# Inverse transform over k2: one F32 product or three 12-bit F32R products, from the seventh group on

## The chip, the cores and the metric

One core of a Trainium2 chip runs the kernel. The metric is the time of one launch on the device in microseconds (us), the median of several runs. The profile is of one execution, taken by the hardware profiler; its times count from the start of its span. Engines: TensorE (PE, with PEld for its weight loads), ScalarE (ACT), VectorE (DVE), GpSimd (POOL), and SyncE (SP), which issues the DMAs.

## The reference

The input x is 2 sequences of 3008 tokens with 256 features. Three layers follow each other:

```python
X = np.fft.rfft(x, axis=1)
Yr = Xr @ w_r - Xi @ w_i + b_r
Yi = Xr @ w_i + Xi @ w_r + b_i
Y = shrink(Yr) + 1j * shrink(Yi)        # towards zero by 0.01
y = np.fft.irfft(Y, n=3008, axis=1)
h = y @ win1;  x1 = (h * cos(h)) @ wout1        # 256 -> 2048 -> 256
h = x1 @ win2; out = (h * clip(h + 3, 0, 6) / 6) @ wout2
```

All inputs and the output are float32 (the weights of the last two layers come as float64).

## The kernel before

**Precision.** Most products on PE are made from split operands. A value is written once to the type F32R (a float with 12 mantissa bits that are kept, the high part), and once as the rest, value minus high part, in F32R too. A product is then three: high x high, high x low, low x high, added in PSUM. Products of the two long transforms over k2 aren't split: both operands are F32, and an F32 product is executed as two passes on PE.

**First phase, to about 165 us.** The transform of 3008 tokens is done in two steps (47 x 64). `a_part` makes the forward step, `w_mm`, `b_mm`, `v_mm` the rest up to `u`, which goes to DRAM (`u_dram`) in 96 rows for each of 32 pairs of columns and both sequences. Meanwhile a converter, spread in small steps between the other work, turns the float64 weights into split F32R tiles: `load` fetches 512 KB into one of two buffers with the tag `raw`, ACT, DVE and POOL work on it, and the last reader of a raw tile is line 169 on DVE. The converter does the second layer's weights during the second phase.

**Inverse step.** A group is four pairs, 376 tokens; there are 16 groups (0 to 15). `load_u(g)` fetches u (96 x 4 x 256) and the table tg (96 x 376) for one group into one buffer each. `y_part(g, ec)` makes one half of the 256 features of the group: four products of 96 rows, 128 x 94 (line 290), into one PSUM tile of the tag `h`, of which there are four buffers. ACT and DVE then write the result as high and low part into the token tiles (lines 304 and 305). After the second half it calls `load_u(g + 1)`. Groups 0 to 2 are done in the first phase, the others in the second.

**Second phase.** The tokens are 12 blocks of up to 512. A unit is 128 of the 2048 hidden features of one block and layer. `mm_h` makes it on PE (line 602, six products of 512 columns into an `h` tile); ACT and DVE apply the function (lines 613, 614, 626, 634, 635 for layer 0, lines 618 and 637 for layer 1) and split it (`gh`, line 645 on ACT, `gl`, line 646 on DVE, which is the last reader of the `h` tile); `mm_out` multiplies it by wout four units later (line 659, six products). Units of layer 0 (even) and layer 1 (odd) alternate, a group of 32 units for each block, so that layer 1 is three blocks behind. In a unit's turn ACT gets, in this order, the first function of this unit, `gh` of the unit two before, the second function of the unit before, and, in layer 0, line 626 of this unit. The order on PE, ACT and SP is the program's; DVE and POOL are put in order by a planner.

**Where the inverse step stands.** The parts of the groups that the next block needs are hung behind units near the end of the present group of units, in a table `events`: the last part three units before the end, the others two units apart in front of it. Four of the 16 groups (7 and 8, 11 and 12) are needed in pairs; the others of the groups 6 to 15 singly.

Of the kernel before, what the change touches and what calls it, by code (L numbers as in the profile page):

```python
# [9 lines left out]
F32 = mybir.dt.float32  # L10
F32R = mybir.dt.float32r
# [3 lines left out]
AF = mybir.ActivationFunctionType  # L15
ALU = mybir.AluOpType
# [5 lines left out]
NB, D, DFF = 2, 256, 2048  # L22
# [4 lines left out]
TP = 2 * N1  # L27
ROWS = 2 * DOF
LAM = 0.01
TWO_PI = 2.0 * math.pi  # L30
YPAIRS = 4
# [3 lines left out]
TILE = 128  # L35
# [9 lines left out]
STAGED = [0] * 9 + [1, 2, 4, 5, 7, 8, 10] + [12] * 10  # L45
YP = (15, 17, 18, 19, 20, 21, 22)
YE = 3


def _split(a):  # L50
# [66 lines left out]
def fourier_moe_moe_kernel(ctx, tc, x, w_r, w_i, b_r, b_i, ta, tg, fg, win1, wout1, win2, wout2, out):  # L117
    nc = tc.nc
    pe, act, dve, sp = nc.tensor, nc.scalar, nc.vector, nc.sync

    def f32(ap):
        return ap.bitcast(F32)

    persist = ctx.enter_context(tc.tile_pool(name="persist", bufs=1))
# [130 lines left out]
    MAXT = max(BLOCK_TOKENS)  # L255
    starts = [sum(BLOCK_TOKENS[:j]) for j in range(NBLK + 1)]
    YT = YPAIRS * TP
    NG = NB * NPAIR // YPAIRS

    def tok0(j):  # L260
# [2 lines left out]
    def groups_of(j):  # L263

        return range(-(-starts[j] // YT), -(-starts[j + 1] // YT))

    u_sb, tg_sb, y_sb, x1_sb = {}, {}, {}, {}


    def token_sets(pool, i, tag):  # L270
# [5 lines left out]
    def load_u(g):  # L276
        if g >= NG:
            return
        b, p0 = divmod(g * YPAIRS, NPAIR)
        ut = persist.tile([ROWS, YPAIRS, D], F32, tag="u_sb", name=f"u_sb{g}")  # L280
        sp.dma_start(ut, u_dram[b][:, :, p0 : p0 + YPAIRS, :].rearrange("s f i e -> (s f) i e"))
        tt = persist.tile([ROWS, -(-YT // TILE) * TILE], F32, tag="tg_sb", name=f"tg_sb{g}")
        sp.dma_start(tt[:, 0:YT], tg[:, p0 * TP : (p0 + YPAIRS) * TP])
        u_sb[g], tg_sb[g] = ut, tt

    def y_part(g, ec):

        yp = psum.tile([128, 512], F32, tag="h", bufs=4, name=f"yp{g}_{ec}")
        for i in range(YPAIRS):
            pe.matmul(  # L290
                yp[:, i * TP : (i + 1) * TP],
                lhsT=u_sb[g][:, i, ec * 128 : (ec + 1) * 128],
                rhs=tg_sb[g][:, i * TP : (i + 1) * TP],
                start=True,
                stop=True,
            )
        for j in range(NBLK):
            t0, t1 = max(g * YT, starts[j]), min((g + 1) * YT, starts[j + 1])
            if t0 < t1:
                if j not in y_sb:  # L300
                    y_sb[j] = free_sets.pop(0)
                yh, yl = (z[:, t0 - starts[j] : t1 - starts[j]] for z in y_sb[j][ec])
                src = yp[:, t0 - g * YT : t1 - g * YT]
                act.activation(yh, src, AF.Copy)  # L304
                dve.tensor_tensor(yl, src, f32(yh), op=ALU.subtract)
        if ec == 1:
            load_u(g + 1)


    with ExitStack() as actx:  # L310
        apool = actx.enter_context(tc.tile_pool(name="apool", bufs=1))
        with tc.manual_schedule(engines={mybir.EngineType.PE, mybir.EngineType.SP, mybir.EngineType.Activation}):
# [238 lines left out]
            for i in range(NB * NP):  # L551
                k2_step(i)
                if i == 0:
                    constants(2)
                if i == YP[0]:
                    free_sets += token_sets(persist, 0, "zt")
                    load_u(0)
                elif i in YP:
                    y_part(*divmod(YP.index(i) - 1, 2))
# [5 lines left out]
    mpool = ctx.enter_context(tc.tile_pool(name="mpool", bufs=1))  # L565
    with tc.manual_schedule(engines={mybir.EngineType.PE, mybir.EngineType.SP, mybir.EngineType.Activation}):
# [5 lines left out]
        order, units, events = [], [], {}  # L572
        for i, group in enumerate(groups):
            g0, n0 = len(units), len(order)
            order += group
            step = 4 if i == 0 else 1
            for q in range(NFC // step):
                units += [(n0 + n, *job, q * step + f) for n, job in enumerate(group) for f in range(step)]
            size = len(units) - g0
            if i + 1 < len(groups) and groups[i + 1][0][0] == 0:  # L580
                parts = [(g, e) for g in groups_of(groups[i + 1][0][1]) for e in range(2)]
                for k, (g, e) in enumerate(reversed(parts)):
                    events.setdefault(g0 + size - YE - 2 * k, []).append(lambda g=g, e=e: y_part(g, e))

        acc, hp_t, gs_t, mid = {}, {}, {}, {}
        w2i, w2o = None, None
# [98 lines left out]
        for g in range(G + DELAY):  # L685
# [22 lines left out]
            if 0 <= g - DELAY < G:  # L708
                n2, m2, _, fc2 = units[g - DELAY]
# [50 lines left out]
```

## Time and profile before

| | |
|---|---|
| three runs | 1225.84, 1227.66, 1229.45 us; median 1227.66 us |
| the profiled execution | 1225.41 us, of which the span from the first to the last instruction is 1223.6 us |
| PE busy | 1216.1 us (99%) |
| DVE, ACT, POOL busy | 803.1, 786.0, 86.1 us |
| granted clock of PE | full in all 40 slices |

The busy times are sums over the span. Matmuls on PE are pipelined: one begins before the one before it has ended, so a matmul's own duration is longer than the distance to the next one's start, and it is the distance that PE's stream is made of.

### The profile page before, as it was taken

To read this page: it belongs to the slowest core of one execution; us is meant where nothing else is said; L and a number is where in the kernel's file an instruction comes from. 1 tells how busy PE (TensorE), PEld (TensorE's weight loads), DVE (VectorE), ACT (ScalarE), POOL (GpSimd) and SP (SyncE) were. 2 spreads that over 40 slices of the span, in tenths; PEclk is the share of its full clock that TensorE was granted. 3 is DMA by queue.
4 is the path that set the end of the run, shared out by engine and by line. 5 is a ranking of instruction groups with operands and counts; after the bars stand their busy time and mean duration, and the time that the engine had idled before them with its cause. 6 is when DMAs were issued, how large, how long until landed. Compare 5 with 4: busy or idle time off the path is not lost.

```text
span 1223.6 us, 15626 instructions
## 1 busy us (share of the span) xinstructions
PE 1216.1 (99%) x5671; PEld 1021.2 (83%) x5673; DVE 803.1 (66%) x1328; ACT 786.0 (64%) x1487; POOL 86.1 (7%) x68
## 2 busy tenths in 40 slices
PE   8999999999999999999999999999999999999998
PEld 7888878888888888888888888888888888888888
DVE  3978789899986655656566556656556656554444
ACT  3667689898776666666666666666666666654443
POOL 0330122222321000000000000000000000000000
PEclk9999999999999999999999999999999999999999
DMA  9633431212200001000001001001001000000000
GB/s 247 190 97 94 129 96 52 70 54 70 69 36 18 18 1 36 18 1 18 18 1 35 1 19 35 1 1 35 1 1 35 1 1 18 1 1 18 18 8 23
DMA packets 25077, 48.47 MB, mean 40 GB/s; under 512 B 2756, under 2 KB 12744, under 8 KB 25000
## 3 DMA queue, kind: packets, MB, share of 16 engines
q1 hardware_dynamic: 25000, 47.48, 13.5%
q8 instruction: 44, 0.72, 0.2%
q14 instruction: 33, 0.27, 0.1%
HBM read 35.02 MB, written 12.45 MB: 39 GB/s over the span
## 4 chain that ended last, share of the span: by engine, by line
PE 95%; DVE 1%; DMA 1%; ACT 1%; issue 0%; SPq 0%; DVEq 0%
PE acc L659 41%; PE h L602 41%; PE pp L422 5%; PE bp L447 3%; PE yp L290 2%; PE zp L349 1%; PE vp L473 1%; DMA x_big<-in_x_dram 1%; DMA x<-in_x_dram 1%; PE bp L442 0%; DVE r L614 0%; DVE h L635 0%; DVE gl L646 0%; SPq L342 0%; SPq L338 0%
## 5 line engine op out<-in xcount | busy, mean ns | idle before, releaser
L637 DVE SCALAR_TENSOR_TENSOR h<-r,h 128x512 f32<-128x512 f32 (+1 forms) x192 | 131.3, 684 | 251.3 <-ACT r L618 251.2
L602 PE MATMUL h<-tok,w1i 128*128 128x512 f32 (+1 forms) x1152 | 291.6, 388 | 1.0 <-DVE gl L646 0.5
L602 PE MATMUL h<-tok,w2i 128*128 128x512 f32 (+1 forms) x1152 | 287.8, 385 | 0.0
L659 PE MATMUL acc<-gh,w1o 128*128 128x512 f32 (+1 forms) x768 | 264.5, 385 | 0.0
L659 PE MATMUL acc<-gh,w2o 128*128 128x512 f32 (+1 forms) x768 | 263.6, 385 | 0.0
L646 DVE TENSOR_TENSOR gl<-h,gh 128x512 fp32r<-128x512 f32 (+1 forms) x384 | 258.0, 672 | 0.6 <-ACT gh L645 0.5
L602 PEld LDWEIGHTS h<-tok,w1i 128*128 128x128 f32 x1152 | 213.1, 188 | 44.1 <-DVE gl L646 2.1
L602 PEld LDWEIGHTS h<-tok,w2i 128*128 128x128 f32 x1152 | 214.8, 188 | 41.0 <-DVE gl L646 0.4
L645 ACT ACTIVATE gh<-h 128x512 fp32r<-128x512 f32 (+1 forms) x384 | 224.5, 585 | 4.8 <-DVE h L635 3.8
L618 ACT ACTIVATE r<-h 128x512 f32<-128x512 f32 (+1 forms) x192 | 113.0, 588 | 172.9 <-PE h L602 172.9
L614 DVE SCALAR_TENSOR_TENSOR r<-r,h 128x512 f32<-128x512 int32 (+1 forms) x192 | 129.5, 675 | 103.3 <-ACT r L613 103.1
L613 ACT ACTIVATE r<-h 128x512 int32<-128x512 f32 (+1 forms) x192 | 113.0, 589 | 130.8 <-PE h L602 129.7
L659 PEld LDWEIGHTS acc<-gh,w1o 128*128 128x128 f32 x768 | 144.0, 188 | 27.9
L659 PEld LDWEIGHTS acc<-gh,w2o 128*128 128x128 f32 x768 | 143.9, 188 | 27.4
L659 PE MATMUL acc<-gl,w1o 128*128 128x512 f32 (+1 forms) x384 | 147.8, 385 | 0.0
L659 PE MATMUL acc<-gl,w2o 128*128 128x512 f32 (+1 forms) x384 | 147.8, 385 | 0.0
L626 ACT ACTIVATE r<-r 128x512 f32<-128x512 f32 (+1 forms) x192 | 119.7, 623 | 42.5 <-DVE r L614 41.7
L635 DVE TENSOR_TENSOR h<-r,h 128x512 f32<-128x512 f32 (+1 forms) x192 | 129.3, 674 | 0.0
L634 ACT ACTIVATE r<-r 128x512 f32<-128x512 f32 (+1 forms) x192 | 120.0, 625 | 0.0
L659 PEld LDWEIGHTS acc<-gl,w1o 128*128 128x128 f32 x384 | 72.1, 188 | 13.9
L659 PEld LDWEIGHTS acc<-gl,w2o 128*128 128x128 f32 x384 | 72.1, 188 | 13.9
L304 ACT ACTIVATE tok<-yp 128x376 fp32r<-128x376 f32 (+22 forms) x54 | 19.2, 356 | 31.1 <-PE yp L290 20.6
(89 smaller groups left out, 907.8 us busy)
## 6 DMA issues: line engine op xcount, KB each, us to landing
u_dram<-v SPq DMA_DIRECT2D x48, 128.0 KB, 2.4
u_sb<-u_dram SPq DMA_DIRECT2D x16, 384.0 KB, 3.8
out_dram<-o SPq DMA_DIRECT2D x22, 256.0 KB, 2.1
x<-in_x_dram SPq DMA_DIRECT2D x11, 384.0 KB, 5.0
raw0i<-in_win_dram SPq DMA_DIRECT2D x8, 512.0 KB, 3.9
raw0o<-in_wout_dram SPq DMA_DIRECT2D x8, 512.0 KB, 4.1
raw1i<-in_win_dram SPq DMA_DIRECT2D x8, 512.0 KB, 3.6
raw1o<-in_wout_dram SPq DMA_DIRECT2D x8, 512.0 KB, 3.7
```

Source lines behind the costliest of these rows:

```text
L422: pe.matmul(pp.rearrange("p a e -> p (a e)"), lhsT=za[:, p, kc, 2 * (k2 % 2) : 2 * (k2 % 2) + 2, :].rearrange("p r n -> p (r n)"), rhs=wb[ ...
L602: pe.matmul(hp[:, :t], lhsT=w[:, c0 : c0 + 128], rhs=r[:, :t], start=(i == 0), stop=(i == 5))
L613: act.activation(k[:, :t], hp[:, :t], AF.Copy, bias=0.0, scale=1.0 / TWO_PI)
L614: dve.scalar_tensor_tensor(r[:, :t], k[:, :t], -TWO_PI, hp[:, :t], op0=ALU.mult, op1=ALU.add)
L618: act.activation(r[:, :t], hp[:, :t], AF.Relu, bias=3.0, scale=1.0)
L626: act.activation(mid[g][:, :t], mid[g][:, :t], AF.Abs)
L634: act.activation(r[:, :t], r[:, :t], AF.Sin, bias=math.pi / 2, scale=-1.0)
L635: dve.tensor_tensor(hp[:, :t], r[:, :t], hp[:, :t], op=ALU.mult)
L637: dve.scalar_tensor_tensor(hp[:, :t], r[:, :t], 6.0, hp[:, :t], op0=ALU.min, op1=ALU.mult)
L645: act.activation(gh[:, :t], hp[:, :t], AF.Copy)
L646: dve.tensor_tensor(gl[:, :t], hp[:, :t], f32(gh[:, :t]), op=ALU.subtract)
L659: pe.matmul(acc[n][d][:, :t], lhsT=w[:, fc % 2, d * 128 : (d + 1) * 128], rhs=r[:, :t], start=(fc == 0 and i == 0), stop=(fc == NFC - 1 an ...
```

## The change

For groups 6 to 15 (`YR = 6`) u and tg are split as other operands are. A new function `split_u(g)` lets ACT write the high parts and POOL the low parts of both: u's into two tiles of the tag `raw`, whose buffers the converter used until then, tg's into two new tiles. Then it calls `load_u(g + 1)`, which for these groups is no longer called by `y_part`. `y_part` makes three F32R products where it made one F32 product: high x high, high x low, low x high, added in PSUM. The events: the two halves of a group stay two units apart; where two groups are needed for a block, the first of them stands 12 units ahead of the second (it was 4); `split_u(g)` stands five units before the group's first half. Groups 0 to 5 are as before.

```diff
+YR = 6
...
+    TGW = -(-YT // TILE) * TILE
...
+    def split_u(g):
+
+        us_sb[g] = [persist.tile([ROWS, YPAIRS, D], F32R, tag="raw", bufs=2, name=f"us{z}_{g}") for z in range(2)]
+        tgs_sb[g] = [mpool.tile([ROWS, TGW], F32R, tag=f"tgs{z}", name=f"tgs{z}_{g}") for z in range(2)]
+        for src, (hi, lo) in ((u_sb[g], us_sb[g]), (tg_sb[g][:, 0:YT], [t[:, 0:YT] for t in tgs_sb[g]])):
+            act.activation(hi, src, AF.Copy)
+            nc.gpsimd.tensor_tensor(lo, src, f32(hi), op=ALU.subtract)
+        load_u(g + 1)
+
     def y_part(g, ec):
 
         yp = psum.tile([128, 512], F32, tag="h", bufs=4, name=f"yp{g}_{ec}")
+        if g < YR:
+            terms = [(u_sb[g], tg_sb[g])]
+        else:
+            (uh, ul), (th, tl) = us_sb[g], tgs_sb[g]
+            terms = [(uh, th), (uh, tl), (ul, th)]
         for i in range(YPAIRS):
-            pe.matmul(
-                yp[:, i * TP : (i + 1) * TP],
-                lhsT=u_sb[g][:, i, ec * 128 : (ec + 1) * 128],
-                rhs=tg_sb[g][:, i * TP : (i + 1) * TP],
-                start=True,
-                stop=True,
-            )
+            for k, (u, t) in enumerate(terms):
+                pe.matmul(
+                    yp[:, i * TP : (i + 1) * TP],
+                    lhsT=u[:, i, ec * 128 : (ec + 1) * 128],
+                    rhs=t[:, i * TP : (i + 1) * TP],
+                    start=(k == 0),
+                    stop=(k == len(terms) - 1),
+                )
...
-        if ec == 1:
+        if ec == 1 and g < YR:
             load_u(g + 1)
...
                 for k, (g, e) in enumerate(reversed(parts)):
-                    events.setdefault(g0 + size - YE - 2 * k, []).append(lambda g=g, e=e: y_part(g, e))
+                    at = g0 + size - YE - (2 * k if g < YR else 2 * (1 - e) + 12 * (k // 2))
+                    events.setdefault(at, []).append(lambda g=g, e=e: y_part(g, e))
+                    if g >= YR and e == 0:
+                        events.setdefault(at - 5, []).append(lambda g=g: split_u(g))
```

## Rows read from the trace of the kernel before

**Rows 1.** The page: the span, and busy time and instructions of each engine.

```profile
span 1223.6 us, 15626 instructions
...
PE 1216.1 (99%) x5671; PEld 1021.2 (83%) x5673; DVE 803.1 (66%) x1328; ACT 786.0 (64%) x1487; POOL 86.1 (7%) x68
```

**Rows 2.** The page: the chain that ended last, by line.

```profile
PE acc L659 41%; PE h L602 41%; PE pp L422 5%; PE bp L447 3%; PE yp L290 2%; PE zp L349 1%; PE vp L473 1%; DMA x_big<-in_x_dram 1%; DMA x<-in_x_dram 1%; PE bp L442 0%; DVE r L614 0%; DVE h L635 0%; DVE gl L646 0%; SPq L342 0%; SPq L338 0%
```

**Rows 3.** The view of line 290: durations min/median/max in ns.

```profile
L290 PEld LDWEIGHTS yp<-tg_sb,u_sb x256: 187/192/192, 126.0 to 1010.4; 96*128 96x128 f32 x128
L290 PE MATMUL yp<-tg_sb,u_sb x256: 244/275/275, 126.2 to 1010.5; 96*128 96x94 f32 x128
```

**Rows 4.** PE in order of time about group 10's first half: start, us.

```profile
643.71 0.39 PE L659 MATMUL acc<-gl,w2o 128*128 128x512 f32 x1
...
644.62 0.39 PE L659 MATMUL acc<-gh,w2o 128*128 128x512 f32 x1
644.85 1.03 PE L290 MATMUL yp<-tg_sb,u_sb 96*128 96x94 f32 x8
645.72 1.66 PE L602 MATMUL h<-tok,w1i 128*128 128x512 f32 x6
647.22 0.39 PE L659 MATMUL acc<-gh,w1o 128*128 128x512 f32 x1
...
648.58 1.52 PE L602 MATMUL h<-tok,w2i 128*128 128x512 f32 x6
649.94 0.39 PE L659 MATMUL acc<-gh,w2o 128*128 128x512 f32 x1
```

**Rows 5.** PE and its weight loads in order of time, 645.26 to 645.95.

```profile
645.26 0.61 PE L290 MATMUL yp<-tg_sb,u_sb 96*128 96x94 f32 x4
...
645.40 0.30 PEld L290 LDWEIGHTS yp<-tg_sb,u_sb 96*128 96x128 f32 x2
645.72 0.30 PEld L602 LDWEIGHTS h<-tok,w1i 128*128 128x128 f32 x2
```

**Rows 6.** DVE in order of time, beside the same part.

```profile
644.98 0.68 DVE L646 TENSOR_TENSOR gl<-h,gh 128x512 fp32r<-128x512 f32 x1
```

**Rows 7.** PE in order of time about a part of the first phase (group 2).

```profile
149.89 1.03 PE L290 MATMUL yp<-tg_sb,u_sb 96*128 96x94 f32 x8
150.70 0.47 PE L422 MATMUL pp<-wh,zh 128*128 128x512 f32 x1
...
152.16 0.40 PE L473 MATMUL vp<-sh,fgr 128*128 128x512 f32 x1
```

**Rows 8.** PE in order of time in the last block: 384 columns.

```profile
1101.31 0.33 PE L659 MATMUL acc<-gh,w1o 128*128 128x384 f32 x1
...
1102.19 0.34 PE L659 MATMUL acc<-gh,w1o 128*128 128x384 f32 x1
```

**Rows 9.** Groups by form: a copy from SBUF on ACT, a subtraction on POOL.

```profile
L173 ACT ACTIVATE w2o<-cva1o 128x512 fp32r<-128x512 f32 x8 | 5.1, 631 | 0.0
...
L176 POOL TENSOR_TENSOR w2o<-cva1o,w2o 128x512 fp32r<-128x512 f32 x8 | 10.4, 1294 | 22.2 <-ACT w2o L173 22.2
```

**Rows 10.** ACT in order of time: idle before and its releaser in brackets.

```profile
643.75 0.60 ACT L618 ACTIVATE r<-h 128x512 f32<-128x512 f32 x1 [0.80 <-PE h L602]
```

**Rows 11.** The view of line 646, from 300 to 376 us.

```profile
L646 DVE TENSOR_TENSOR gl<-h,gh x28: 676/683/692, 302.1 to 375.6; 128x512 fp32r<-128x512 f32 x28
```

**Rows 12.** DVE, POOL and PE in order of time before group 6's first half.

```profile
358.31 0.69 DVE L169 SCALAR_TENSOR_TENSOR cvb1o<-raw1o,cvb1o 128x512 f32<-128x512 uint32 x1
...
369.19 0.69 DVE L169 SCALAR_TENSOR_TENSOR cvb1o<-raw1o,cvb1o 128x512 f32<-128x512 uint32 x1
...
370.02 1.31 POOL L170 TENSOR_TENSOR cva1o<-cva1o,cvb1o 128x512 f32<-128x512 f32 x1 [8.33 <-DVE cvb1o L169]
...
375.49 1.03 PE L290 MATMUL yp<-tg_sb,u_sb 96*128 96x94 f32 x8
```

**Rows 13.** The page: DMA issues, the load of u.

```profile
u_sb<-u_dram SPq DMA_DIRECT2D x16, 384.0 KB, 3.8
```

More of the change, by code (lines that the diff above doesn't have):

```diff
@@ L267, in fourier_moe_moe_kernel @@
     u_sb, tg_sb, y_sb, x1_sb = {}, {}, {}, {}
+    us_sb, tgs_sb = {}, {}
     def token_sets(pool, i, tag):
@@ L281, in load_u @@
         sp.dma_start(ut, u_dram[b][:, :, p0 : p0 + YPAIRS, :].rearrange("s f i e -> (s f) i e"))
-        tt = persist.tile([ROWS, -(-YT // TILE) * TILE], F32, tag="tg_sb", name=f"tg_sb{g}")
+        tt = persist.tile([ROWS, TGW], F32, tag="tg_sb", name=f"tg_sb{g}")
         sp.dma_start(tt[:, 0:YT], tg[:, p0 * TP : (p0 + YPAIRS) * TP])
         u_sb[g], tg_sb[g] = ut, tt
+    def split_u(g):
[5 more added lines that the diff above has]
+        load_u(g + 1)
     def y_part(g, ec):
         yp = psum.tile([128, 512], F32, tag="h", bufs=4, name=f"yp{g}_{ec}")
-        for i in range(YPAIRS):
-            pe.matmul(
-                yp[:, i * TP : (i + 1) * TP],
-                lhsT=u_sb[g][:, i, ec * 128 : (ec + 1) * 128],
-                rhs=tg_sb[g][:, i * TP : (i + 1) * TP],
-                start=True,
-                stop=True,
-            )
+        if g < YR:
[3 more added lines that the diff above has]
+            terms = [(uh, th), (uh, tl), (ul, th)]
+        for i in range(YPAIRS):
+            for k, (u, t) in enumerate(terms):
[6 more added lines that the diff above has]
+                )
         for j in range(NBLK):
```

## The prediction

> **What bounds the kernel.** I read the page's first lines: TensorE (PE) is busy for 1216.1 of 1223.6 us [rows 1]. Then the chain that ended last: PE's lines L659 and L602 are 82% of it, and the line the change rewrites, L290, 2% [rows 2]. So nearly every microsecond added to PE's stream is added to the end, and one taken from it is won only if nothing else holds PE at that place. L290 shows 256 PE instructions for 16 groups x 2 halves x 4 = 128 products: an F32 product is two passes of 94 columns, each with a weight load [rows 3].
>
> Next I read one part's place in order of time: group 10's first half, between two groups of six at L602 [rows 4]. Its eight passes start at 644.85, the next L602 matmul at 645.72: 0.87 us. The six matmuls there take 1.50 (645.72 to 647.22), where the six at 648.58 take 1.36 (to 649.94). A part thus costs 0.87 + 0.14 = 1.01 us. The pace of the passes is that of the weight loads: two loads in a row span 0.30 at about 0.19 each, so start to start is 0.11, and four passes of 0.275 span 0.61, so 0.112 from start to start [rows 3, 5]. Two loads of L602, which are F32R, span 0.30 too: an F32R load isn't faster.
>
> Then VectorE. The gl of L646 runs 644.98 to 645.66 [rows 6], and L602's next matmul and weight load start together at 645.72 [rows 4, 5]. gl ends the use of an h buffer in PSUM, and a part takes a fifth tile from these four buffers. So after its last pass PE waits some 0.06 us for gl, though no view lists it (PE is still counted busy). The first six parts show the case without gl: the eighth pass starts about 0.75 after the first (1.03 less 0.275) [rows 3, 7], the next matmul 0.81 after the first (149.89 to 150.70), and the six after it take 1.46 (to 152.16) [rows 7]. From a part's first pass to the end of the next six that is 2.27, against 2.37 (644.85 to 647.22) here. The gate costs 0.10 us a part. It also sets a floor: shorter products would leave L602 at 645.72.
>
> **The change part by part.** *Products.* For groups 6 to 15, in 2 halves each, so 20 parts, 8 passes become 4 x 3 = 12 passes of F32R with 94 columns. No row of before shows an F32R product under 384 columns. Bounds: from above, 0.176 at 384 columns (1101.31 to 1102.19 in five) [rows 8], unless a narrow F32R product goes as an F32 one does, 2 x 0.112 = 0.224. From below, the line through 384 (0.176) and 512 columns (0.228: 643.71 to 644.62 in four [rows 4]) carried down to 94 columns gives 0.176 - 290 x 0.052/128 = 0.06. In between lies 0.11, at which F32R loads follow each other [rows 5]; since every product here loads its own 128 columns of weights, and the three terms reload uh rather than keep it (PE has 5673 loads for 5671 matmuls [rows 1], though L602 uses weights twice in a row), I take 0.112. That products accumulate into the same 94 columns costs nothing at this pace: the two F32 passes do so now.
>
> Sum for a part: four more passes x 0.112 = +0.45, first pass to next matmul 0.81 + 0.45 = 1.26, and the six after it 1.46; together 2.72 for today's 2.37. That is +0.35: 0.45 less the gate's 0.10, since L602 then asks for its buffer at 646.11, after gl's 645.66. Twenty parts: +7.0 us. With the bounds: with p a product's pace, the first pass to the next matmul is 0.81 + 12p - 8 x 0.112 = 12p - 0.09, and the change a part is that + 1.46 - 2.37: at 0.176, +1.11, in all +22; at 0.224, +1.69, +34; at 0.06 the gate holds, +0.
>
> The Trainium skill, "TensorE: Matmul & The Clock Gate", section LDWEIGHTS, says that a weight load's time goes by its columns, columns / 1.2 in ns, whatever the contraction: 107 ns here. By that page an estimate of the sum is 20 x 4 x 0.107 = 8.5 us less the gate: the trace's 0.112 agrees, and the rule speaks against trading two loads for three.
>
> *Splits.* Ten times ScalarE copies 1024 and 376 elements. A copy from SBUF takes 0.63 at 512 [rows 9], so these at most 1.26 and 0.63, 1.89 together. They stand behind L626 of an even unit, and before the next instruction, L618 of the odd unit, ScalarE is idle for 0.80, until PE has ended L602 [rows 10]. So 0.80 is covered, and L618, the gh behind it and the gl that frees an h buffer come up to 1.1 later. What covers that: gl ends 1.9 us after L618's start (643.75 to 645.66 [rows 6, 10]), and without a part in between PE asks for that buffer only after the six products of L659 (1.36) and the whole next unit (647.22 to 649.94, 2.72 [rows 4]), some 4 us after L618's release, which leaves 2 us. Bound: 0 to 1.1 a split, 0 to 11 us; I take 0, as the 2 us are more. GpSimd subtracts 1024 and 376 elements; at 1.29 for 512 [rows 9] at most 2.6 and 1.3. Copies and subtractions take at most 5.8 us, and the part follows five units or 5 x 2.72 = 13.6 us later: covered. GpSimd costs VectorE nothing that I can see: a gl takes 0.683 in the median while GpSimd converts [rows 11], and 0.68 where it is idle [rows 6].
>
> *Buffers.* The halves of u go into the converter's raw buffers. Before group 6 the last raw tile is read until 369.88 (369.19 + 0.69), and the split is due five units before the part, near 362. The copy uses the older buffer, last read at 359.0 (358.31 + 0.69); GpSimd's first subtraction waits to 369.9, and at 3.9 both end at 373.8, or at 376.5 if two operations of the conversion (from 370.02, 1.31 and 1.29) go first. The part starts at 375.49 [rows 9, 12]: 0 to 1.0 us, once. I take 0, as the subtractions are due first. Behind GpSimd's wait stand only the last conversions.
>
> *Loads.* The next group's load moves from behind a part to behind its split, 12 units or more ahead of use, and takes 3.8 us [rows 13]. On SP it waits for GpSimd, and the next output stores behind it are far off. Nothing.
>
> *Moved parts.* Where a block needs two groups, the first's parts move 8 units earlier, behind an odd unit as now; the same gate, the same cost. Nothing.
>
> So 1225.41 + 7.0 = 1232.4 for the profiled execution; it lies 2.25 under the median 1227.66, and the forecast for a median is 1234.7.
>
> **Rivals.** *A. The forecast*, 0.112 a product: +7.0; own range with the scatter of the three runs, 1231 to 1238. Chance 0.74.
>
> *B. No change*, the other side: if a narrow F32R product goes at its columns' rate (0.06), the part ends before gl, and L602 starts at 645.72 as now. It decides from 12p - 0.09 under 0.87, so p under 0.08: 1227.7. For it: the line through 384 and 512 columns. Against it: loads at 0.11 after each other. Chance 0.10. [...]
>
> *C. Narrow F32R is dearer than its load*, 0.176 to 0.224: +22 to +34, 1250 to 1262. For it: no row shows F32R so narrow. Against it: the F32 passes reach 0.112. Chance 0.08.
>
> *D. The splits stall PE*: ScalarE's 1.1 passes on to PE by gl at half or more of the 10 splits: +7.0 and 5 to 11, 1240 to 1246. It decides where gl comes over 2 us late. For it: ScalarE runs in order, and gh stands behind the copies. Against it: those 2 us. Chance 0.08.
>
> **How the numbers follow.** A measurement of this kernel tells 0.3%, 3.7 us, from no change. A, C and D are slower except for an edge of A; of B a fifth could be measured as faster. Slower 0.87, same 0.10, faster 0.03. The range leaves out C, most of B and the far end of D: 1230 to 1243.
>
> **What would show it.** L290 in groups 6 to 15 with 240 instead of 160 passes, each shorter than the 0.275 of now, starts 0.11 apart, 1.26 from a part's first pass to L602, six at L602 in 1.46 and 0.35 more from part to part. B: L602 still starts 0.06 after gl. C: starts 0.176 or more apart. D: PE idle before L602 with gl late, or before L290 in group 6 with GpSimd as what ended it. The forecast is wrong if F32R loads of 94-column products don't follow each other at 0.11.

## The result

The changed kernel takes 1235.91 us (median of 14 runs), the kernel before 1228.72 us (median of 14), a ratio of 1.0065 with a 95% interval of 1.0051 to 1.0079. It is slower by 7.2 us; the forecast was 7.0 us, 1234.7 us for the median and 1230 to 1243 as its range. Of the 1.2 us between 1234.7 and 1235.91, 1.06 are there because the kernel before has a median of 1228.72 here and had 1227.66 in the three runs that the forecast started from.

The page of the changed kernel, as [rows 1, 2] of before; line 680 is what was 659, 623 was 602, 308 was 290, 667 was 646:

```profile
span 1235.6 us, 15858 instructions
...
PE 1227.2 (99%) x5751; PEld 1031.8 (84%) x5753; DVE 804.3 (65%) x1328; ACT 798.7 (65%) x1507; POOL 119.8 (10%) x88
...
PE acc L680 41%; PE h L623 40%; PE pp L440 5%; PE yp L308 3%; PE bp L465 3%; PE zp L367 1%; PE vp L491 1%; DMA x_big<-in_x_dram 1%; DMA x<-in_x_dram 1%; PE bp L460 0%; DMA tg_sb<-in_tg_dram 0%; DVE r L635 0%; DVE h L656 0%; DVE gl L667 0%; SPq L360 0%
```

PE has 80 matmuls more, 20 parts of 12 instead of 8, as many more loads, and it still sets the end. This execution's span is 12.0 us longer than that of before, and not all of that is the change: PE in order of time at the first part that the change touches (group 6's first half):

```profile
380.17 0.39 PE L680 MATMUL acc<-gh,w2o 128*128 128x512 f32 x1
380.40 1.44 PE L308 MATMUL yp<-tgs,us 96*128 96x94 f32 x12
```

Its first pass starts at 380.40, in before at 375.49 [rows 12]. So 4.9 us were lost earlier, and all of it by 142.9 us, long before the first instruction that the change touches (the copy on ScalarE at 367.53). PE, early in the changed kernel's span (367 was 349, 440 was 422):

```profile
23.32 1.91 PE L367 MATMUL zp<-ta,x 96*128 96x96 f32 x8 [1.86 <-DMA x<-in_x_dram]
...
27.96 0.63 PE L440 MATMUL pp<-wl,zh 128*128 128x512 f32 x1
28.39 0.63 PE L440 MATMUL pp<-wh,zl 128*128 128x512 f32 x1
```

PE had waited 1.86 us for x (1.39 at the same place in before), and from 23.3 to 30 us its granted clock was 0.51, about the lower of its two levels (1.2 of 2.4 GHz), where it was 1.00 in before: products of L440 start 0.43 apart, the same ones in before 0.23. By then 3.6 us are lost; the rest is lost by 142.9 us, where PE waited 0.9 us for a load of tg. A later run with the same splits and buffers, e8 below, has a granted clock of 1.00 in those stretches and starts that part at 376.33. From that part's first pass to the span's end the changed kernel takes 855.2 us, before 848.1: 7.1 us for 20 parts, 0.355 each. The runs of before scatter in the same way: beside e1 to e4, 13 of them with a mean granted clock of 0.997 took 1229.9 us in the mean, 7 with 1.0 took 1226.9.

One part, the counterpart of [rows 4 to 6]: PE, its weight loads and VectorE in order of time at group 10's first half, then the view of line 308 as in [rows 3].

```profile
652.61 1.44 PE L308 MATMUL yp<-tgs,us 96*128 96x94 f32 x12
653.88 1.61 PE L623 MATMUL h<-tok,w1i 128*128 128x512 f32 x6
655.34 0.40 PE L680 MATMUL acc<-gh,w1o 128*128 128x512 f32 x1
...
653.51 0.41 PEld L308 LDWEIGHTS yp<-tgs,us 96*128 96x128 f32 x3
...
652.75 0.68 DVE L667 TENSOR_TENSOR gl<-h,gh 128x512 fp32r<-128x512 f32 x1
```

```profile
L308 PEld LDWEIGHTS yp<-tgs,us x240: 188/192/192, 380.2 to 1022.6; 96*128 96x128 f32 x120
L308 PE MATMUL yp<-tgs,us x240: 208/274/276, 380.4 to 1022.6; 96*128 96x94 f32 x120
```

Three loads span 0.41 at 0.19 each: 0.11 from start to start, the pace of before. The first pass to L623 takes 1.27 (0.87 in before), the six matmuls there 1.46 (1.50): 2.73 against 2.37, 0.36 a part. All 20 parts of the changed kernel take 2.73, those of before 2.36 to 2.38. gl is over at 653.43, and L623 starts 0.45 later: it waits no more.

### The profile page after: what moved, and what is told of

The parts are those of the page before. It is cut to its first block, busy times and chain, and to the rows that moved or that the text cites. A ratio compares the mean times of both kernels' runs of the same rounds, so it can differ in the third digit from the quotient of the medians.

```text
span 1235.6 us, 15858 instructions
## 1 busy us (share of the span) xinstructions
PE 1227.2 (99%) x5751; PEld 1031.8 (84%) x5753; DVE 804.3 (65%) x1328; ACT 798.7 (65%) x1507; POOL 119.8 (10%) x88
## 4 chain that ended last, share of the span: by engine, by line
PE 95%; DMA 2%; DVE 1%; ACT 1%; issue 0%; SPq 0%; DVEq 0%
PE acc L680 41%; PE h L623 40%; PE pp L440 5%; PE yp L308 3%; PE bp L465 3%; PE zp L367 1%; PE vp L491 1%; DMA x_big<-in_x_dram 1%; DMA x<-in_x_dram 1%; PE bp L460 0%; DMA tg_sb<-in_tg_dram 0%; DVE r L635 0%; DVE h L656 0%; DVE gl L667 0%; SPq L360 0%
## 5 line engine op out<-in xcount | busy, mean ns | idle before, releaser
L658 DVE SCALAR_TENSOR_TENSOR h<-r,h 128x512 f32<-128x512 f32 (+1 forms) x192 | 131.4, 684 | 255.1 <-ACT r L639 255.0
L623 PE MATMUL h<-tok,w1i 128*128 128x512 f32 (+1 forms) x1152 | 290.6, 388 | 1.0 <-DVE gl L667 0.5
L623 PE MATMUL h<-tok,w2i 128*128 128x512 f32 (+1 forms) x1152 | 287.9, 385 | 0.0
L623 PEld LDWEIGHTS h<-tok,w1i 128*128 128x128 f32 x1152 | 213.2, 188 | 43.9 <-DVE gl L667 2.3
L623 PEld LDWEIGHTS h<-tok,w2i 128*128 128x128 f32 x1152 | 214.8, 188 | 41.0 <-DVE gl L667 0.4
L639 ACT ACTIVATE r<-h 128x512 f32<-128x512 f32 (+1 forms) x192 | 112.8, 587 | 164.1 <-PE h L623 164.1
L295 POOL TENSOR_TENSOR us<-u_sb,us 96x1024 fp32r<-96x1024 f32 x10 | 24.1, 2406 | 592.8 <-ACT us L294 592.2
```

Of the source, the lines that this page charges most:

```text
L623: pe.matmul(hp[:, :t], lhsT=w[:, c0 : c0 + 128], rhs=r[:, :t], start=(i == 0), stop=(i == 5))
L639: act.activation(r[:, :t], hp[:, :t], AF.Relu, bias=3.0, scale=1.0)
L658: dve.scalar_tensor_tensor(hp[:, :t], r[:, :t], 6.0, hp[:, :t], op0=ALU.min, op1=ALU.mult)
```

## The experiments

Each ran beside the kernel before on the same chip; the medians of before were 1229.04 us beside e1 to e4 and 1228.62 us beside e5 to e8.

**e1: the splits alone.**

```diff
-        if g < YR:
+        if True:
             terms = [(u_sb[g], tg_sb[g])]
...
-        load_u(g + 1)
...
-        if ec == 1 and g < YR:
+        if ec == 1:
             load_u(g + 1)
```

> The splits, the raw buffers and the moved parts stay as in the change, but the products are the F32 ones of before (8 passes a part), and the load of the next group stands behind the part again. Theory (all of the +7 us is 4 more passes a part): as before, 0 us within 1.5, and each part from its first pass to the end of the next six matmuls takes 2.37 us. Rival (the copies on ScalarE hold up gl, or group 6 waits for GpSimd): 5 to 11 us over before, with PE waiting behind the splits.

Measured: 1229.48 us, ratio 1.0004 (0.9992 to 1.0015). PE at group 10's first half:

```profile
646.58 1.02 PE L307 MATMUL yp<-tg_sb,u_sb 96*128 96x94 f32 x8
647.45 1.67 PE L622 MATMUL h<-tok,w1i 128*128 128x512 f32 x6
648.96 0.39 PE L679 MATMUL acc<-gh,w1o 128*128 128x512 f32 x1
```

A part takes 0.87 to the next matmul and 1.51 for its six, as before. The copies, subtractions, buffers and moved places cost nothing that can be measured; the rival's 5 to 11 us are outside the interval. The moved load is not in this run, which puts it back behind the part.

**e2: one product of the three.**

```diff
-            terms = [(uh, th), (uh, tl), (ul, th)]
+            terms = [(uh, th)]
```

> Only the product high x high is left of the three (the two others are left out, so the output is coarser): 4 passes a part instead of 12. Theory (gl frees the buffer that L602 needs, at 0.87 us after a part's first pass at the soonest): a part costs what it did before, 2.37 us to the end of the next six; the time is that of before, 0 us within 1.5. Rival (only the passes count): 8 x 0.112 x 20 = 18 us less than the changed kernel, 11 less than before, a ratio of 0.991.

Measured: 1229.61 us, ratio 1.0001 (0.9991 to 1.0011). Leaving out 8 of 12 passes gave back the 7 us of the change and nothing more. PE, then VectorE, in order of time at the same part:

```profile
648.92 0.54 PE L308 MATMUL yp<-tgs,us 96*128 96x94 f32 x4
649.80 1.67 PE L623 MATMUL h<-tok,w1i 128*128 128x512 f32 x6 [0.33 <-DVE gl L667]
651.30 0.39 PE L680 MATMUL acc<-gh,w1o 128*128 128x512 f32 x1
...
649.06 0.68 DVE L667 TENSOR_TENSOR gl<-h,gh 128x512 fp32r<-128x512 f32 x1
```

The passes are half as many as in before, and L623 still starts 0.88 after the first of them, 0.06 after the end of gl (649.74). The wait that no view listed in before now stands in brackets, since PE has run dry.

**e3: products of twice the width.**

```diff
+            w = 1 if g < YR else 2
+            c = min(i, YPAIRS - w)
...
-                    yp[:, i * TP : (i + 1) * TP],
+                    yp[:, c * TP : (c + w) * TP],
...
-                    rhs=t[:, i * TP : (i + 1) * TP],
+                    rhs=t[:, c * TP : (c + w) * TP],
```

> As the change, but each of the 12 products of a part streams 188 columns instead of 94 (of neighbouring columns, so the sums are not those wanted); the weight loads are as many. Theory (the pace is that of the weight loads, 0.112): the time of the changed kernel, +7 us to before, starts 0.11 apart. Rival (the stream counts: 94 more columns at 0.0004 us each, 0.038 a product): 12 x 0.038 x 20 = 9 us more, +16 to before.

Measured: 1237.60 us, ratio 1.0067 (1.0051 to 1.0083), as the changed kernel. PE at the same part:

```profile
652.73 1.48 PE L310 MATMUL yp<-tgs,us 96*128 96x188 f32 x12
654.04 1.58 PE L625 MATMUL h<-tok,w1i 128*128 128x512 f32 x6
655.46 0.40 PE L682 MATMUL acc<-gh,w1o 128*128 128x512 f32 x1
```

1.31 + 1.42 = 2.73, to the hundredth the 2.73 of 94 columns. Twice the stream costs nothing: the streams lie under the loads.

**e4: the kernel before, with gh ahead of L618.** All products and F32 passes stay.

```diff
+                if g >= 2 and m == 1 and g <= max(events):
+                    split_g(g - 2)
                 act1(g)
-            if 0 <= g - 2 < G:
+            if 0 <= g - 2 < G and not (g < G and units[g][1] == 1 and g <= max(events)):
                 split_g(g - 2)
```

> The kernel before, with one order changed: in layer 1's units ScalarE makes gh of the unit two before ahead of L618, in the time in which it waited for L602. Theory (a part is held by gl for 0.10 us): gl comes before the part's last pass, L602 starts 0.81 after the first pass instead of 0.87, its six take 1.46, so 20 parts x 0.10 = 2.0 us less than before, ratio 0.998. Rival (the 0.10 is what it costs PE to go from F32 to F32R, not a wait): the time and the 0.87 and 1.50 of before.

Measured: 1227.31 us, ratio 0.9991 (0.9973 to 1.0008): the 2 us expected are less than these runs can tell from nothing. The trace tells it: PE, ScalarE and VectorE at the same part.

```profile
648.04 1.03 PE L290 MATMUL yp<-tg_sb,u_sb 96*128 96x94 f32 x8
648.85 1.63 PE L602 MATMUL h<-tok,w1i 128*128 128x512 f32 x6
650.32 0.40 PE L659 MATMUL acc<-gh,w1o 128*128 128x512 f32 x1
...
646.05 0.58 ACT L645 ACTIVATE gh<-h 128x512 fp32r<-128x512 f32 x1
646.94 0.60 ACT L618 ACTIVATE r<-h 128x512 f32<-128x512 f32 x1 [0.31 <-PE h L602]
...
646.66 0.69 DVE L646 TENSOR_TENSOR gl<-h,gh 128x512 fp32r<-128x512 f32 x1 [0.58 <-ACT gh L645]
```

gh now lies in ScalarE's wait for PE, gl ends 0.69 before the part's first pass, and the same eight F32 passes are followed by L602 after 0.81 instead of 0.87, whose six take 1.47 instead of 1.50: 2.28 for 2.37. So the 0.10 was the wait for gl, not a price of going from F32 to F32R.

**e5: e2 and e4 together.** The edits are those two.

> Only high x high of the three products, as in e2_one_term, and gh ahead of L618 in layer 1's units, as in e4_before_gh_first. Theory (4 passes less than before show once gl is early): from a part's first pass to L602 0.81 - 4 x 0.112 = 0.36, six in 1.46, 1.82 for 2.37 of before: 20 x 0.55 = 11 us less than before, ratio 0.991. Rival (something besides gl holds L602, or F32R's first passes are dearer): no more than the 2 us of e4_before_gh_first.

Measured: 1217.43 us, ratio 0.9917 (0.9901 to 0.9934). PE at the same part:

```profile
641.65 0.54 PE L308 MATMUL yp<-tgs,us 96*128 96x94 f32 x4
642.03 1.61 PE L623 MATMUL h<-tok,w1i 128*128 128x512 f32 x6
643.49 0.40 PE L680 MATMUL acc<-gh,w1o 128*128 128x512 f32 x1
```

0.38 + 1.46 = 1.84 for 2.37 of before, 20 x 0.53 = 10.6 us, measured 11.2. The four passes that were worth nothing in e2 are worth 9 us once gl is early: some 12 us lie between e2 and e5, of which e4's order alone gives 2 by its trace. This kernel is faster than both, but it leaves out the low parts, so it is no substitute at their precision.

**e6: the changed kernel with gh ahead of L639 (L618 of before).** The edit is that of e4.

> The changed kernel with gh ahead of L618. Theory (gl came 0.35 us before the 12 passes were over, so the gate no longer binds there): as the changed kernel, +7 us to before within 1.5. Rival (gl still holds a part of it): 2 us less than the changed kernel.

Measured: 1236.46 us, ratio 1.0075 (1.0060 to 1.0089). A part takes 1.27 to L623 and 1.45 for its six, as in the changed kernel. Twelve passes outlast gl in either order, so the order is worth nothing here.

**e7: two products of three, gh ahead.** The terms are (uh, th) and (uh, tl).

> High x high and high x low (low x high left out), gh ahead of L618: 8 F32R passes a part, each of one stream where F32's pass has the slower one. Theory (the pace is the loads', so 8 F32R passes cost what 8 of F32 do): as e4_before_gh_first, 2 us less than before, ratio 0.998, starts 0.112 apart. Rival (F32R's passes are cheaper): 8 x 0.05 x 20 = 8 us less than e4_before_gh_first.

Measured: 1227.43 us, ratio 0.9992 (0.9982 to 1.0002), 1.2 us under before, where e4 was 1.7 under it on another chip; each lies in the other's interval. PE at the same part:

```profile
648.70 0.99 PE L308 MATMUL yp<-tgs,us 96*128 96x94 f32 x8
649.53 1.62 PE L623 MATMUL h<-tok,w1i 128*128 128x512 f32 x6
650.99 0.39 PE L680 MATMUL acc<-gh,w1o 128*128 128x512 f32 x1
```

Eight F32R passes take 0.83 to the next matmul and 2.29 to the end of the six, e4's eight of F32 0.81 and 2.28. A pass of either kind costs the same, within 0.01 us a part.

**e8: a third of the loads with half the columns, gh ahead.**

```diff
+                c = 64 if k == 1 else 128
                 pe.matmul(
-                    yp[:, i * TP : (i + 1) * TP],
-                    lhsT=u[:, i, ec * 128 : (ec + 1) * 128],
+                    yp[0:c, i * TP : (i + 1) * TP],
+                    lhsT=u[:, i, ec * 128 : ec * 128 + c],
```

> The changed kernel with gh ahead of L618, and the middle product (high x low) made for 64 of the 128 features alone, so that its weight load has 64 columns; the other 64 features go without that product. Theory (a load's time goes by its columns): 4 of a part's 12 loads fall from 0.112 to 0.056, 0.22 a part, 4.5 us less than e6_change_gh_first, +2.5 to before. Rival (a pass has a fixed cost of 0.11, whatever it loads): as e6_change_gh_first, +7 to before.

Measured: 1231.76 us, ratio 1.0038 (1.0020 to 1.0057), 4.7 us less than e6. PE at the same part:

```profile
646.84 1.22 PE L309 MATMUL yp<-tgs,us 96*128 96x94 f32 x12
647.90 1.61 PE L624 MATMUL h<-tok,w1i 128*128 128x512 f32 x6
```

Still 12 passes of 94 columns, but 1.06 to the next matmul for 1.27: four loads of 64 columns saved 0.21, 0.053 each, so such a load takes 0.112 - 0.053 = 0.06. The recorded duration of a load fell with it, from 0.192 to 0.138 in the mean. The Trainium skill, "TensorE: Matmul & The Clock Gate", section LDWEIGHTS, lets a load's time go by its columns; these runs agree, with 0.06 at 64 and 0.11 at 128.

## Why the prediction was right, point by point

*The products.* Forecast: four more passes at 0.112, 1.26 to L602's next matmul, six in 1.46, +0.35 a part. Measured: 1.27, 1.46, +0.36, over the 20 parts 7.1 us in the traces and 7.2 in the medians. The pace was right for the reason given: doubling the stream did nothing (e3), halving a load's columns halved its share (e8), and F32 and F32R passes cost the same by the piece (e4, e7). Rival C fell with the changed kernel's own trace.

*Loads and moved parts.* Forecast: nothing. The moved parts are in e1, at +0.4 us. No run takes the moved load out by itself, but 20 parts at 0.36 are the whole 7.1 us, which leaves nothing for it.

*The gate.* Forecast: gl costs 0.10 a part in before and sets a floor at 0.87. e4 shows the 0.10, e2 the floor, e5 that nothing else holds L602 down to four passes, and e6 that the change had already outgrown it. So of the 0.45 that four passes cost, 0.10 was paid from the wait. That makes rival B half right: cheaper products would have left the time as it was, but these are not cheaper.

*The splits.* Forecast: covered. The copies took 1.04 and 0.50, less than the bounds of 1.26 and 0.63. ScalarE in order of time ahead of group 10, and VectorE's next two instructions:

```profile
639.20 0.64 ACT L647 ACTIVATE r<-r 128x512 f32<-128x512 f32 x1 [0.27 <-DVE r L635]
639.74 1.04 ACT L294 ACTIVATE us<-u_sb 96x1024 fp32r<-96x1024 f32 x1
640.69 0.50 ACT L294 ACTIVATE tgs<-tg_sb 96x376 fp32r<-96x376 f32 x1
641.09 0.58 ACT L639 ACTIVATE r<-h 128x512 f32<-128x512 f32 x1
...
641.70 0.70 DVE L658 SCALAR_TENSOR_TENSOR h<-r,h 128x512 f32<-128x512 f32 x1 [1.93 <-ACT r L639]
642.31 0.68 DVE L667 TENSOR_TENSOR gl<-h,gh 128x512 fp32r<-128x512 f32 x1
...
652.14 0.70 DVE L658 SCALAR_TENSOR_TENSOR h<-r,h 128x512 f32<-128x512 f32 x1 [1.49 <-ACT r L639]
```

L639 starts without a gap behind the copies, and L658 waited for it 1.93 where it waits 1.49 with no copies ahead (the last line, ahead of group 10's part): gl comes 0.44 late, inside the 2 us that were counted as cover, so rival D's condition isn't met. e1 puts a number to it: +0.4 us, within what can't be told from none.

*Group 6's buffers.* Forecast: GpSimd can begin at 369.9 and is done by 373.8 to 376.5, against a part at 375.49. It came nearer than the value I took, 0 for "the subtractions are due first": VectorE and GpSimd in order of time (4.9 us later than before, as said).

```profile
376.29 1.67 DVE L170 SCALAR_TENSOR_TENSOR cvb1o<-raw1o,cvb1o 128x512 f32<-128x512 uint32 x1
...
376.12 1.29 POOL L177 TENSOR_TENSOR w2o<-cva1o,w2o 128x512 fp32r<-128x512 f32 x1 [6.07 <-ACT w2o L174]
378.04 2.40 POOL L295 TENSOR_TENSOR us<-u_sb,us 96x1024 fp32r<-96x1024 f32 x1 [0.63 <-DVE cvb1o L170]
```

The last read of a raw tile ended at 377.96, 3 us later than before's 369.88 and the 4.9 say (1 us of it is the longer L170, told of below), and u's low part was ready at 380.44, between the 378.7 and 381.4 that the forecast's two ends give with the 4.9. The part's first pass started at 380.40, and only its third, whose weights load some 0.1 later, needs the low part. PE lost nothing, by less than a tenth of a microsecond. The value of 0 was right and its reason was not: u's subtraction did not go first, it stood behind the conversion's L177 and waited for L170, and what saved the 0 was that the low part comes third. That was luck.

*What I had wrong without effect.* I expected each F32R pass to show less than F32's 0.275. Its median is 0.274. In every part the first pass, whose weights were loaded before, shows 0.208 (0.244 with F32, 0.250 with e3's 188 columns), and all others 0.27 to 0.28; behind e8's loads of 64 columns they show 0.22. So a recorded duration holds the wait for its own load, and only a part's first pass gives away the shorter stream. And "GpSimd costs VectorE nothing that I can see" held for gl, which reads PSUM, but not for L170 above.

## What to carry to other kernels

For products with few columns (94 here) count weight loads, not streams: F32's two passes a product and F32R's three went by their loads, 0.11 each, and an F32R product could have had twice its columns for nothing (e3). Before paying for shorter work on the busiest engine, look what frees the buffer that its next instruction writes; PE was "busy" 99%, and yet halving a part's passes was worth nothing until gl came earlier. Where such a gate stands, an order on another engine (here gh into ScalarE's idle time) has to come first.

## What the runs showed of the hardware

VectorE's instruction that combines two tiles in SBUF (L170, line 169 before) took 1.67 us while GpSimd's subtraction of 376.12 ran beside it, against 0.69 at 358.31 and 369.19 in before [rows 12]. Before has the same at another place, GpSimd and VectorE in order of time:

```profile
182.44 1.29 POOL L176 TENSOR_TENSOR w1i<-cva0i,w1i 128x512 fp32r<-128x512 f32 x1 [9.19 <-ACT w1i L173]
182.67 1.61 DVE L169 SCALAR_TENSOR_TENSOR cvb0i<-raw0i,cvb0i 128x512 f32<-128x512 uint32 x1
```

Of the 32 times that before runs L169, three have GpSimd beside them and take 1.61 to 1.62; the other 29 take 0.67 to 0.69. gl, which reads one tile in PSUM and one in SBUF, wasn't lengthened [rows 11]. The Trainium skill, "GPSIMD Engine Reference", section Key points, says that GpSimd shares its SBUF interfaces with VectorE and that instructions with two SBUF inputs, or in a mode that takes two ports, contend; L169 and L170 agree with it, at about 0.95 us each, but no run here was made to take GpSimd's work away from them.

Two inputs in SBUF aren't needed for it. L166, which reads one tile in SBUF and writes one there, takes 0.43 at 368.72 in before, with GpSimd idle, and 1.45 here, GpSimd and VectorE in order of time; in which mode it ran, no view tells.

```profile
316.58 1.29 POOL L176 TENSOR_TENSOR w2i<-cva1i,w2i 128x512 fp32r<-128x512 f32 x1 [7.13 <-ACT w2i L173]
316.71 1.45 DVE L166 TENSOR_SCALAR cvb1i<-cva1i 128x512 uint32<-128x512 uint32 x1
```
